# Causal attention and a gated MLP on one core: score maxima taken bank by bank, and a table that ranks every operation of the list schedule

## The chip, the cores and the metric

The kernel runs on one core of a Trainium2 chip. The metric is device time in microseconds of one execution. Three runs of the kernel before gave 362.40, 362.74 and 361.01 us, median 362.4. PE is TensorE (matmuls), DVE is VectorE, ACT is ScalarE, POOL is GpSimd, SP is the engine that issues the DMAs.

## What is computed

Four batches, twelve heads of 64, 448 tokens. Attention is causal; its output is the input x (448 x 768 per batch) of a gated MLP:

```python
scores = q @ k.T / sqrt(64);  scores[mask] = -1e9
attn = exp(scores - max);  attn = attn / sum;  x = attn @ v     # per head
h = gelu(x @ w_in);  u, v = h[..., :512], h[..., 512:]           # tanh gelu, 768 -> 1024
v_n = (v - mean) / sqrt(var + 1e-6) * g_ln
v_s = w_sg @ v_n + b_sg                                           # over tokens, 448 x 448
out = x + (u * v_s) @ w_out                                       # 512 -> 768
```

## The kernel before

The work is cut into operations of one to about ten instructions. Each is recorded by `od.add` with its engine, a modelled duration, what it reads and writes, and a number `at`. When all are recorded, `Order.plan` (line 157) makes a list schedule of them: it keeps a modelled clock for each engine, and when an engine is free it takes, of the operations that the model calls ready, the one with the lowest `at`. The instructions are then emitted in that order, and each engine runs its own instructions strictly in it; what an engine waits for is set by semaphores on the chip, not by the model. `STAY` (line 83) is added to `at` where PE would have to change the shape of its matmuls.

- **Pairs.** 24 pairs of heads, six per batch (`pair`, line 500). A pair loads q and k, and PE makes scores for four chunks of query rows (`CH`, line 24) in two groups: chunks 3 and 0 into one PSUM bank per head, chunks 2 and 1 into another (`GROUPS`). DVE adds the mask in place and takes the row maxima (`mxs`, line 528, eight per pair), ACT takes the exponentials with row sums (line 538, ten per pair), and DVE and a small PE transpose make the reciprocals of the sums, which go through DRAM to be spread (`rd`, `rb`). The exponentials are transposed: in pairs 0 to 7 by PE (`tx`, `ty`, line 585), then copied to SBUF by ACT or DVE (`evict`); from pair 8 on by DVE (line 573) and four DMAs. Then PE multiplies by v (`PV`, line 616), DVE scales the result (`scale`, line 646), and `keep_x` splits it into two parts for the MLP with ACT or POOL and POOL.
- **MLP.** Per batch (`mlp`, line 694), every operand is split in two parts and each product takes three matmuls. One operation of `group` (line 669) is three matmuls (`CUT`), for the token groups and the u groups those of one pair's x. First four token groups (`m<-win,x`, 512 columns), then four u groups (`m<-x,win`), four groups over tokens (`m<-wsg,vn`), and six output groups (`m<-g,wout`). Behind each stand gelu and normalisation on ACT, DVE and POOL. An operation that opens a PSUM bank for the MLP may run early (`EARLY = 2` of them) before all it needs is there.
- **Weights.** w_in comes in twelve pieces as 64-bit numbers and is converted by ACT (line 453), DVE (lines 455 and 457) and POOL (lines 460 and 461); w_out likewise in sixteen.
- **Start.** DVE clears a buffer (`warm`, line 422) and PE does seven matmuls on it (line 427) ahead of the first scores; DVE also clears constants (`consts2`, lines 407 to 413).
- **End.** The last output group of the last batch is added and stored in two halves (`cuts`).

What sets the order before is about a hundred numbers: `STEP`, `MLP`, `LEN`, `PAIR` and `DUE`, from which each operation's `at` is computed.

Of the kernel before, what the change touches and what calls it, by code (L numbers as in the profile page):

```python
# [23 lines left out]
CH = {  # L24
    3: (128, 448, 0, 0, 320),
    0: (64, 64, 0, 448, 0),
    2: (128, 320, 1, 192, 192),
    1: (128, 192, 1, 0, 64),
}
# [23 lines left out]
WO = 192  # L53

GROUPS = (3, 0), (2, 1)

WARM, FILL, EARLY = 7, 0, 2

# [10 lines left out]
    S=(351.19, -329.08, 282.5, 225.63), mx=(-8.77, -147.73, 166.31, -265.1),  # L69
# [10 lines left out]


TICK, BUSY, SHIFT = 10.24 / 3, 3400, 0.12
STAY = 286.72
MOVE = 0.62
FULL = 128, 128
COLD = 6.0, 1.35


def due(k, b):
    d = DUE[k]  # L90
    return d[b] if isinstance(d, tuple) else d
# [15 lines left out]
class Order:  # L107
# [49 lines left out]
    def plan(self):  # L157
# [61 lines left out]
        def when(n):  # L219
            t = rdy[n]  # L220
            for k, tag in enumerate(ops[n]["shr"]):
                if len(avail[tag]) <= k or len(avail[None]) <= k:
                    return 1e9
                if n in wants and stuck(n):
                    opened[:] = [m for m in opened if stuck(m)]
                    if len(opened) >= self.early[tag]:
                        return 1e9
                t = max(t, sorted(avail[tag])[k], sorted(avail[None])[k])
            return t
# [19 lines left out]
        while len(order) < len(ops):  # L249
# [10 lines left out]
            tops = [(ops[n]["at"], n) for n in banks if when(n) <= s + 1e-6] + [q[0] for q in now.values() if q]  # L260
            at, n = min(tops, key=lambda x: (x[0] + (STAY if e == "pe" and (ops[x[1]]["shape"] == FULL) != (shape == FULL) else 0.0), x[1]))
            o = ops[n]
# [18 lines left out]
            if e == "sp":  # L281

                moved = max(moved, end + 0.65) + o["size"] * (COLD[1] if end < COLD[0] else 1.0)
                done = moved + 1.5
# [29 lines left out]
def attention_gated_mlp(ctx: ExitStack, tc: tile.TileContext, qk, vP, w_in, g_ln, w_sgT, b_sg, w_out, out):  # L314
    nc = tc.nc
    B, HP, D, S = vP.shape[0], vP.shape[1], vP.shape[4] // 2, qk.shape[3]
# [24 lines left out]
    def bank(tag):  # L341
        return Buf(ps, [128, 512], F32, tag, "b")
# [4 lines left out]
    mask = const.tile([128, S], BF16, name="mask")  # L347
    mask2 = const.tile([128, 320], BF16, name="mask2")
# [18 lines left out]
    od = Order(slots, BANKS, 8, dict(m=EARLY))  # L367
# [5 lines left out]
    def pe(dur, fn, r, w, at, shape=FULL, rows=1.0):  # L373
        od.add("pe", dur, fn, r, w, at, shape=shape, rows=rows)
# [4 lines left out]
    def dve(n, fn, r, w, at, rate=1.0417, done=0.0, port=False, ring=()):  # L379
        od.add("dve", 0.068 + n * rate / 1000, fn, r, w, at, done, port=port, ring=ring)  # L380
# [4 lines left out]
    def start(p):  # L385
        b, h = divmod(p, HP)
        return sum(STEP[:b]) * HP + STEP[min(b, B - 1)] * h
# [112 lines left out]
    def pair(p):  # L500
        b, hp = divmod(p, HP)
        T = start(p) + PAIR[p]
# [3 lines left out]
        s = [[bank("s") for k in range(2)] for z in range(2)]  # L506
# [4 lines left out]
        def score(cs):  # L511
            for c in cs:
                m, n, bk, col, q0 = CH[c]
                w = 128 if m == 128 else 66
                for z in range(2):
                    r = slice(64 * z, 64 * z + 64)
                    nc.tensor.matmul(out=s[z][bk].t[0:w, col:col + n], lhsT=qk_.t[r, 0, q0:q0 + w],  # L517
                                     rhs=qk_.t[r, 1, 0:n], start=True, stop=True)
        for cs in GROUPS:
            pe(sum(CH[c][1] * 4 / 2400 + 0.036 for c in cs), lambda cs=cs: score(cs), [qk_],  # L520
               [s[z][CH[cs[0]][2]] for z in range(2)], T + due("S", b), (64, 128))


        for c in (3, 0, 2, 1):
            m, n, bk, col, _ = CH[c]
            mk = mask2 if c == 2 else mask[:, S - n:S] if m == 128 else mask[0:m, S - 128:S - 64]
            for z in range(2):
                def mxs(c=c, m=m, n=n, bk=bk, col=col, z=z, mk=mk):
                    o = s[z][bk].t[0:m, col:col + n]
                    nc.vector.tensor_tensor_reduce(out=o, in0=o, in1=mk, scale=-0.125, scalar=3e38, op0=ALU.add,  # L530
                                                   op1=ALU.min, accum_out=ngm[ib[z]][c][0:m])
                dve(n + {0: 45, 1: 45, 2: 10, 3: 5}[c], mxs, ["mask"], [s[z][bk], ("ngm", ib[z], c)], T + due("mx", b), done=0.1)
        ip = p % NS
        for k, (c, r0, k0, n, off, kc) in enumerate(EX):
            m, _, bk, col, _ = CH[c]
# [284 lines left out]
    for b in range(B):  # L820
        for h in range(HP):
            pair(b * HP + h)
        if b == 0:
            weights_b()
        mlp(b)
    with tc.manual_schedule():
        od.run()

# [41 lines left out]
```

## Time and profile before

| | |
|---|---|
| median of three runs | 362.4 us |
| the profiled execution, its own time | 362.34 us |
| its span, first to last instruction | 360.6 us |
| PE busy | 341.9 us, 95% |
| DVE busy | 258.1 us, 72% |
| ACT busy | 200.8 us, 56% |
| POOL busy | 146.9 us, 41% |
| DMA, mean | 193 GB/s |

Busy time is the union of an engine's instructions. A matmul counts as busy until its modelled end, so a busy PE may still be slowed. The page cuts the span into forty slices of about 9 us, and other views give the same for any stretch, by line, by engine or in order of time. Time outside the span is 1.7 us.

### The profile page before, as it was taken

What the parts mean: (1) busy time and instruction counts of PE and PEld (TensorE: products, weight loads), DVE (VectorE), ACT (ScalarE), POOL (GpSimd) and SP (SyncE); (2) the same over time, 40 slices, a digit from 0 to 9 for tenths busy, and PEclk for the clock granted to TensorE, in tenths of its full rate; (3) what the DMA queues carried; (4) which work ended last, traced back from release to release, by engine and by line L of the source; (5) the groups of instructions that cost most, each with busy time, mean ns of one, the idle gap of its engine ahead of it and who ended that gap; (6) DMA issues with size and microseconds to landing.
All of it is one profiled execution on the core that took longest, in us unless ns stands there. A gap on an engine that the chain in (4) does not pass through costs nothing.

```text
span 360.6 us, 6952 instructions
## 1 busy us (share of the span) xinstructions
PE 341.9 (95%) x2231; PEld 271.3 (75%) x2231; DVE 258.1 (72%) x801; ACT 200.8 (56%) x658; POOL 146.9 (41%) x185
## 2 busy tenths in 40 slices
PE   7797999899999999899999989999999999999995
PEld 3464655577889778688978678776888898889994
DVE  6689898699999878738278977778976551286521
ACT  3999999794676186363147855454761600245210
POOL 2227785647557863003421831104235700333630
PEclk9699999899999999999999999999999999999999
DMA  7958999797766547896049589896751668400023
GB/s 243 339 170 264 294 293 336 264 333 220 227 180 211 145 127 189 254 282 192 2 131 273 157 238 273 266 287 187 199 157 31 164 175 246 154 2 0 0 77 128
DMA packets 37972, 69.50 MB, mean 193 GB/s; under 512 B 3888, under 2 KB 18992, under 8 KB 37936
## 3 DMA queue, kind: packets, MB, share of 16 engines
q1 hardware_dynamic: 37936, 69.06, 63.0%
q8 instruction: 18, 0.29, 0.3%
q14 instruction: 18, 0.15, 0.1%
HBM read 39.68 MB, written 12.58 MB: 145 GB/s over the span
## 4 chain that ended last, share of the span: by engine, by line
PE 71%; DVE 10%; DMA 9%; ACT 5%; SPq 3%; issue 1%; DVEq 0%; ACTq 0%
PE m L677 46%; PE o L616 11%; PE s L517 9%; DVE s L530 4%; ACT P L538 3%; DMA B<-P 3%; DMA res<-xd 3%; SPq L577 2%; PE tx L585 2%; PE ty L585 2%; DVE P L573 1%; DMA qk<-in_qk_dram 1%; DMA vraw<-in_vP_dram 1%; DMA xd<-xt 1%; DVE ngm L530 1%
## 5 line engine op out<-in xcount | busy, mean ns | idle before, releaser
L538 ACT ACTIVATE P<-s,ngm 64x64 f32<-64x64 f32 (+3 forms) x240 | 100.2, 426 | 33.5 <-DVE ngm L530 31.4
L530 DVE CUSTOM_DVE_ANT_0 s<-s,mask 128x448 f32<-128x448 f32 (+2 forms) x192 | 75.4, 445 | 12.0 <-PE s L517 11.7
L677 PE MATMUL m<-g,wout 128*128 128x448 f32 x288 | 62.0, 370 | 0.2 <-ACT P L538 0.2
L677 PE MATMUL m<-win,x 128*128 128x512 f32 (+1 forms) x264 | 61.9, 392 | 0.0
L677 PE MATMUL m<-x,win 128*128 128x448 f32 x288 | 60.4, 367 | 0.0
L677 PEld LDWEIGHTS m<-x,win 128*128 128x128 f32 x288 | 53.7, 188 | 5.0 <-issue 0.5
L677 PEld LDWEIGHTS m<-g,wout 128*128 128x128 f32 x288 | 53.0, 188 | 5.7 <-ACT P L538 0.6
L677 PEld LDWEIGHTS m<-win,x 128*128 128x128 f32 (+1 forms) x264 | 47.9, 183 | 11.8
L658 POOL TENSOR_TENSOR x<-xt,x 128x448 fp32r<-128x448 f32 x24 | 27.8, 1167 | 67.1 <-ACT x L657 63.6
L517 PE MATMUL s<-qk 64*128 64x192 f32 (+3 forms) x384 | 54.7, 408 | 0.4 <-DVE tmp L778 0.4
L616 PE MATMUL o<-B,vraw 128*64 128x64 f32 (+4 forms) x672 | 48.3, 293 | 3.3 <-DMA B<-P 1.9
L573 DVE STREAM_TRANSPOSE P<-P 128x1024 f32<-128x1024 f32 x32 | 39.2, 1229 | 14.6 <-DMA B<-P 13.0
L517 PEld LDWEIGHTS s<-qk 64*128 64x128 f32 (+1 forms) x384 | 32.6, 178 | 22.1 <-issue 13.0
L538 ACT ACTIVATION_READ_ACCUMULATOR P<-s,ngm 128x1 f32 (+1 forms) x240 | 47.6, 198 | 0.0
L616 PEld LDWEIGHTS o<-B,vraw 128*64 128x64 f32 x672 | 33.6, 137 | 18.1 <-issue 5.6
L677 PE MATMUL m<-wsg,vn 128*128 128x448 f32 x176 | 36.8, 366 | 0.0
L677 PEld LDWEIGHTS m<-wsg,vn 128*128 128x128 f32 x176 | 32.9, 188 | 2.8 <-issue 0.2
L808 DVE TENSOR_TENSOR res<-m,res 128x448 f32<-128x448 f32 (+1 forms) x25 | 14.7, 598 | 24.8 <-PE m L677 14.1
L731 POOL TENSOR_TENSOR mv<-mv,mhalf 128x1 f32<-128x1 f32 (+1 forms) x16 | 9.1, 570 | 52.3 <-DVE mv L729 52.3
L688 ACT ACTIVATE tmp<-tmp 128x448 f32<-128x448 f32 (+2 forms) x32 | 19.1, 605 | 18.1 <-DVE tmp L686 18.0
L657 ACT ACTIVATE x<-xt 128x448 fp32r<-128x448 f32 x18 | 10.1, 574 | 29.4 <-DVE xt L646 27.2
L530 DVE DVE_READ_ACCUMULATOR2_ANT ngm<- 128x1 f32 (+1 forms) x192 | 26.0, 135 | 0.0
(72 smaller groups left out, 385.7 us busy)
## 6 DMA issues: line engine op xcount, KB each, us to landing
B<-P SPq DMA_DIRECT2D x64, 256.0 KB
qk<-in_qk_dram SPq DMA_DIRECT2D x24, 448.0 KB
vn<-in_w_in_dram SPq DMA_DIRECT2D x12, 512.0 KB
vraw<-in_vP_dram SPq DMA_DIRECT2D x24, 256.0 KB
rb<-rd SPq DMA_DIRECT2D x24, 256.0 KB
xd<-xt SPq DMA_DIRECT2D x24, 224.0 KB
res<-xd SPq DMA_DIRECT2D x12, 448.0 KB
out_dram<-res SPq DMA_DIRECT2D x9, 448.0 KB
```

The costliest lines, as they stand in the source:

```text
L517: nc.tensor.matmul(out=s[z][bk].t[0:w, col:col + n], lhsT=qk_.t[r, 0, q0:q0 + w], rhs=qk_.t[r, 1, 0:n], start=True, stop=True)
L530: nc.vector.tensor_tensor_reduce(out=o, in0=o, in1=mk, scale=-0.125, scalar=3e38, op0=ALU.add, op1=ALU.min, accum_out=ngm[ib[z]][c][0:m])
L538: act(n, lambda c=c, m=m, r0=r0, k0=k0, n=n, bk=bk, col=col, off=off, kc=kc, i=i, z=z: nc.scalar.activation(out=P[i][r0:m, off:off + n], i ...
L573: dve(PW, lambda z=z: nc.vector.transpose(A[ia][:, :, :, z, :].rearrange("p g t k -> p t g k"), P[ib[z]]), Pk[z] + ["P"], Ak, Tt, 1.105)
L585: nc.tensor.transpose(out, P[ib[z]][:, col:col + 128], ident)
L616: nc.tensor.matmul(out=dst(o.t[r]), lhsT=vr.t[:, c, r], rhs=src(z), start=first and n == 0, stop=last and n == len(lst) - 1)
L657: act(S, lambda: nc.scalar.activation(out=y.t[:, 0:S], in_=x.t, func=AF.Copy), [x], [y], Ty, True)
L658: pool_tt(S, lambda: nc.gpsimd.tensor_tensor(out=y.t[:, S + 64:], in0=x.t, in1=f(y.t)[:, 0:S], op=ALU.subtract), [x, y], [(y, 1)], Ty)
L677: nc.tensor.matmul(out=ps.t[0:l().shape[1], 0:n], lhsT=l(), rhs=rr(), start=(k == 0), stop=(k == len(mms) - 1))
L688: act(n, lambda: nc.scalar.activation(out=z(), in_=z(), func=AF.Tanh, scale=GS * GC), [], [t], at, True)
L731: od.add("pool", 0.46, lambda mv=mv, m=m: nc.gpsimd.tensor_tensor(out=mv.t[0:m, 1:2], in0=mv.t[0:m, 1:2], in1=mhalf[0:m], op=ALU.pow), ["s ...
L808: dve(hi - lo, lambda rr=rr, ps=ps, z=z, lo=lo, hi=hi: nc.vector.tensor_tensor(out=rr.t[:, z, lo:hi], in0=ps.t[:, lo:hi], in1=rr.t[:, z, l ...
```

## The change

Two edits. The maxima of a pair are recorded bank by bank and head by head with the narrow chunk first (`MX`): chunk 0 then 3 of head 0, then of head 1, then chunk 1 then 2 likewise. And after all operations are recorded, `at` of each is replaced by its place in a table of all 1926 of them, `ORDER`; `STAY` becomes 0. The numbers that made `at` before no longer decide anything but the numbering. The planner's model and its rules of readiness, buffers and banks stay.

```diff
+MX = (0, 3), (1, 2)
...
-STAY = 286.72
+STAY = 0.0
...
+ORDER = (
+    0, 1, 83, 11, 117, 127, 3, 2, 171, 17, 4, 23, 5, 6, 347, 7, 161, 8, 9, 10, 84, 85, 88, 12, 86, 13, 87, 215, 90,
...
+)
...
-               [s[z][CH[cs[0]][2]] for z in range(2)], T + due("S", b), (64, 128))
+               [s[z][k] for k in sorted({CH[c][2] for c in cs}) for z in range(2)], T + due("S", b), (64, 128))
...
-        for c in (3, 0, 2, 1):
-            m, n, bk, col, _ = CH[c]
-            mk = mask2 if c == 2 else mask[:, S - n:S] if m == 128 else mask[0:m, S - 128:S - 64]
-            for z in range(2):
+        for cs in MX:
+            for z, c in [(z, c) for z in range(2) for c in cs]:
+                m, n, bk, col, _ = CH[c]
+                mk = mask2 if c == 2 else mask[:, S - n:S] if m == 128 else mask[0:m, S - 128:S - 64]
...
+    for k, n in enumerate(ORDER):
+        od.ops[n]["at"] = k
```

Each score group wrote one bank per head already, so the third edit changes nothing. No operation is added or removed. Lines of the changed kernel are 101 to 104 higher than before, behind the table.

**DVE, start of the program.** Before:

```order
L422 MEMSET tmp 128x512
L407 MEMSET P_90 128x64 x4
L407 MEMSET P_91 128x64 x4
L407 MEMSET P_92 128x64 x4
...
L412 MEMSET mhalf 128x1
L413 MEMSET wsg 64x448
L530 ISA s,ngm_96<-s,mask 128x448
```

Now:

```order
L508 MEMSET P_90 128x64 x4
L508 MEMSET P_91 128x64 x4
L508 MEMSET P_92 128x64 x4
...
L513 MEMSET mhalf 128x1
L514 MEMSET wsg 64x448
L523 MEMSET tmp 128x512
L632 ISA s,ngm_97<-s,mask 64x64
```

The clearing of `tmp`, on which the seven first matmuls of PE wait, moved behind all fourteen rows of constants.

**PE, around the scores of pair 5** (`o<-B,vraw` is PV, `s<-qk` scores, `tx` and `ty` transposes, `m<-win,x` the MLP's token groups). Before:

```order
L616 MATMUL o<-B,vraw 64x320 x2
L616 MATMUL o<-B,vraw 64x64 x2
L616 MATMUL o<-B,vraw 64x128 x2
L616 MATMUL o<-B,vraw 64x64 x2
L552 MATMUL s<-ident,rs 8x128
L517 MATMUL s<-qk 128x448 x2
L517 MATMUL s<-qk 66x64 x2
L517 MATMUL s<-qk 128x320 x2
L517 MATMUL s<-qk 128x192 x2
```

Now:

```order
L718 MATMUL o<-B,vraw 64x64 x2
L779 MATMUL m<-win,x 128x512 x3
L654 MATMUL s<-ident,rs 8x128
L618 MATMUL s<-qk 128x320 x2
L618 MATMUL s<-qk 128x192 x2
L687 MATMUL tx<-ident,P_91 128x2x64
L687 MATMUL tx<-ident,P_91 128x128 x3
L687 MATMUL ty<-ident,P_91 128x2x64
L687 MATMUL ty<-ident,P_91 128x128 x3
L779 MATMUL m<-win,x 128x512 x3
L718 MATMUL o<-B,vraw 64x448 x2
```

Matmuls of the first MLP now stand between the parts of pairs 2 to 7. Before, the first of them stands behind PV of pair 7; now 72 of the token groups and 24 of the u groups stand ahead of it.

**PE, where the first MLP goes from its third kind of group to its fourth.** Before:

```order
L616 MATMUL o<-B,vraw 64x64 x4
L552 MATMUL s<-ident,rs 8x128
L677 MATMUL m<-g,wout 128x448 x6
L517 MATMUL s<-qk 128x448 x2
L517 MATMUL s<-qk 66x64 x2
L677 MATMUL m<-g,wout 128x448 x12
```

Now:

```order
L779 MATMUL m<-wsg,vn_1476 128x448 x2
L779 MATMUL m<-g,wout 128x448 x6
L618 MATMUL s<-qk 128x448 x2
L618 MATMUL s<-qk 66x64 x2
L618 MATMUL s<-qk 128x320 x2
L618 MATMUL s<-qk 128x192 x2
L654 MATMUL s<-ident,rs 8x128
L779 MATMUL m<-g,wout 128x448 x39
```

PV of pairs 10 and 11, which stood ahead of the first `m<-g,wout`, moved behind 60 of its 72 matmuls, together.

## Rows read from the trace of the kernel before

**Rows 1.** The page: busy time, share of span, instructions.

```profile
PE 341.9 (95%) x2231; PEld 271.3 (75%) x2231; DVE 258.1 (72%) x801; ACT 200.8 (56%) x658; POOL 146.9 (41%) x185
```

**Rows 2.** Stretches: span, busy us (instructions) of each engine, granted clock, DMA share, GB/s.

```profile
8.00:75.00 67.00, 58.69 (x439) 37.36 (x436) 55.44 (x217) 63.60 (x232) 37.01 (x42) 0.92 0.85 283
74.70:120.00 45.30, 45.30 (x271) 38.13 (x269) 44.53 (x122) 28.94 (x91) 30.67 (x46) 1.00 0.72 216
0.00:126.40 126.40, 116.26 (x792) 82.20 (x792) 109.06 (x383) 95.86 (x326) 75.57 (x105) 0.96 0.79 251
120.00:150.00 30.00, 28.27 (x224) 21.56 (x224) 22.62 (x77) 14.84 (x56) 14.14 (x17) 1.00 0.67 194
205.00:250.00 45.00, 42.40 (x292) 33.03 (x292) 33.83 (x104) 24.33 (x88) 11.27 (x13) 1.00 0.86 250
```

**Rows 3.** In order of time, first 9 us: start, duration, what [idle before it <-releaser].

```profile
0.91 0.48 DVE L422 MEMSET tmp<- 128x512 uint32 x1 [0.91 <-PEq L859]
...
3.54 0.43 DVE L413 MEMSET wsg<- 64x448 f32 x1
...
5.84 0.63 DVE L530 CUSTOM_DVE_ANT_0 s<-s,mask 128x448 f32<-128x448 f32 x1 [1.87 <-PE s L517]
...
1.45 3.17 PE L427 MATMUL m<-tmp 128*128 128x512 bf16 x7 [1.45 <-DVE tmp L422]
...
4.55 3.84 PE L517 MATMUL s<-qk 64*128 64x448 f32 x32
...
7.46 0.63 ACT L538 ACTIVATE P<-s,ngm 128x448 f32<-128x448 f32 x1 [3.83 <-DVE ngm L530]
```

**Rows 4.** By line: names, shapes xcount | busy us, mean ns | idle before <-releasers. ACT.

```profile
L538 ACT ACTIVATE P<-s,ngm 64x64 f32<-64x64 f32 (+3 forms) x240 | 100.2, 426 | 33.5 <-DVE ngm L530 31.4 <-DVE P L573 0.5 <-PE m L677 0.2
...
L592 ACT ACTIVATE B<-tx 128x512 f32<-128x512 f32 x16 | 9.5, 595 | 1.7 <-PE tx L585 1.6
...
L453 ACT ACTIVATE vn<-vn 128x512 f32<-128x512 f32 x12 | 8.0, 680 | 0.1
...
L453 ACT ACTIVATE g<-g 128x192 f32<-128x192 f32 x16 | 5.3, 378 | 1.5 <-DMA g<-in_w_out_dram 0.9 <-POOL wout L461 0.6
...
L688 ACT ACTIVATE tmp<-tmp 128x448 f32<-128x448 f32 (+2 forms) x32 | 19.1, 605 | 18.1 <-DVE tmp L686 18.0
```

**Rows 5.** In order of time: the last copy of pair 7 on ACT, then PE.

```profile
69.64 0.60 ACT L592 ACTIVATE B<-ty 128x512 f32<-128x512 f32 x1
...
71.62 2.08 PE L616 MATMUL o<-B,vraw 128*64 128x448 f32 x24
```

**Rows 6.** By line: PE, the token groups, the u groups, the scores and PV.

```profile
L677 PE MATMUL m<-win,x 128*128 128x512 f32 (+1 forms) x264 | 61.9, 392 | 0.0
...
L677 PE MATMUL m<-x,win 128*128 128x448 f32 x288 | 60.4, 367 | 0.0
...
L517 PE MATMUL s<-qk 64*128 64x192 f32 (+3 forms) x384 | 54.7, 408 | 0.4 <-DVE tmp L778 0.4
...
L616 PE MATMUL o<-B,vraw 128*64 128x64 f32 (+4 forms) x672 | 48.3, 293 | 3.3 <-DMA B<-P 1.9 <-DMA xd<-xt 1.0
```

**Rows 7.** Stretches at half clock, columns as in rows 2.

```profile
11.30:18.10 6.80, 5.71 (x24) 4.13 (x23) 4.00 (x18) 6.67 (x29) 1.93 (x2) 0.50 0.87 317
65.90:69.30 3.40, 3.40 (x15) 2.38 (x16) 1.72 (x8) 1.75 (x8) 3.32 (x4) 0.50 0.51 149
```

**Rows 8.** DVE: by line, the transposes; in order of time, the fourth gcol step.

```profile
L573 DVE STREAM_TRANSPOSE P<-P 128x1024 f32<-128x1024 f32 x32 | 39.2, 1229 | 14.6 <-DMA B<-P 13.0 <-ACT P L538 1.6
...
125.72 0.68 DVE L778 SCALAR_TENSOR_TENSOR tmp<-m,gcol,bB 128x448 f32<-128x448 f32 x1
```

**Rows 9.** One line on DVE: count, min/median/max ns, first and last start; then POOL by line.

```profile
L455 DVE TENSOR_SCALAR g<-g x16: 213/350/875, 78.4 to 118.4; 128x192 int32<-128x192 int32 x16
L455 DVE TENSOR_SCALAR vn<-vn x12: 379/420/1367, 10.1 to 76.3; 128x512 int32<-128x512 int32 x12
...
L461 POOL TENSOR_TENSOR win<-vn,win 128x512 fp32r<-128x512 f32 x12 | 16.7, 1389 | 0.9
```

95 rows, old and new, of the table ORDER are left out of this document.

## The prediction

> **What bounds the kernel now.** The page says PE, 95% busy [rows 1], but that is an average over stages with different limits, so I read the stretches next [rows 2]. From 8 to 75 us, while pairs 0 to 7 go through, PE is busy 58.69 of 67 us and ACT 63.60: ACT is the engine without room, and PE waits for its exponentials and copies. From 74.7 to 120 us, the first MLP, PE is full but so is DVE, 44.53 of 45.3 us. Only after that do both ACT and DVE have room, and what PE still loses there is 1.73 us between 120 and 150 and 2.60 us between 205 and 250. So the kernel has about 8 us of idle PE in a stretch where it has no matmuls that may run, and behind it a stretch that DVE would not let run much faster. Last come the lines of ACT and PE, which give prices [rows 4, 6], and the first microseconds in order of time [rows 3].
>
> **The change, part by part.** The sum is made against the profiled execution, 362.34 us, a span of 360.6 us and 1.7 us around it; the median of the runs is 362.4 us, the same. A difference of 0.5%, 1.8 us, is about what the measurement can tell from none.
>
> *Start: 2.5 us later.* The constants on DVE take from 1.39 us, where the clearing of `tmp` ends, to 3.97 us, 2.58 us [rows 3]. They now come first, so PE's first matmul moves from 1.45 to about 4.0 us. Its seven take 3.1 us to the first score, which moves from 4.55 to 7.1 us. DVE's first maximum moves from 5.84 to 8.4 us. There the narrow chunk goes first; two maxima of 64 columns and one step of weight unpacking (at least 0.379 us [rows 9]) stand ahead of the first wide one. I take ACT's first exponential at 10.0 us instead of 7.46. This is the price of one moved operation, and nothing hides it, as ACT is the limit next.
>
> *Pairs 0 to 7: 9.8 us ahead at their end.* Ahead of the last copy of pair 7, ACT now has 92 exponentials, 26 copies, 4 weight pieces like copies, 11 conversions of w_in (the twelfth falls into ACT's wait at the start), 10 of w_out and 6 gelu steps of the MLP. From the rows [rows 4]: 92 x 100.2/240 = 38.4, 30 x 0.595 = 17.9, 11 x 8.0/12 = 7.3, 10 x 5.3/16 = 3.3, 6 x 0.605 = 3.6, together 70.5 us. The same count for the kernel before (87, 30 and 10) gives 60.9 us from 7.46 us, so 68.4 us, where the trace has 70.24 [rows 5]: ACT waited 1.9 us. With that wait the change ends there at 10.0 + 70.5 + 1.9 = 82.4 us, and PV of pair 7, which before ended 3.5 us behind this copy (at 73.70 us [rows 5]), ends at 85.9 us. By then PE has also done 72 matmuls of the token groups and 24 of the u groups, which before came afterwards: 72 x 61.9/264 + 24 x 60.4/288 = 16.9 + 5.0 = 21.9 us [rows 6]. Before, the same work was done at 73.7 + 21.9 = 95.6 us. PE has the room: its 8.3 idle us, and the second stretch at half clock. In that stretch, 65.9 to 69.3 us, the granted clock is 0.50, that is 1.2 instead of 2.4 GHz, and PE before it had waited and done scores and transposes [rows 7]; half of 3.4 us is lost. The first such stretch, 11.3 to 18.1 us, comes before any MLP matmul can run, and stays.
>
> *First MLP: DVE takes part of the lead back.* Up to the end of the fourth `tmp<-m,gcol` step of the first MLP (line 778), at 126.4 us [rows 8], DVE was busy 109.06 us and idle 17.3 [rows 2]. In the change DVE has the same work ahead of that step but for the transposes of pair 11 (2 x 1.229 us [rows 8]) and some 0.6 us of maxima: 106.0 us. Of the idle time 5.4 us cannot go: 0.9 at the start and 4.5 between the last start-up clearing (now at 4.0 us) and the first maximum. So the bound for this step is 111.4 us. Between that and no lead at all lies the other 14.5 us of DVE's idle time, of which 11.6 fell between 8 and 75 us, where DVE waited for ACT's pace. As ACT stays the limit there I let half remain, 7.3 us: the step ends at 118.7, 7.7 us earlier. That is less than the 9.8 of PE, so DVE decides. But PE then owes work that before was done: PV of pair 10 (48.3/24 = 2.0 us) and scores of pair 12 (54.7/24 = 2.3 us) [rows 6]. What is left is 3.4 us. Ends: nothing to 10.7 us (111.4).
>
> *Later stages: 2.2 us.* PV of pairs 10 and 11, and later 13 and 14, 16 and 17, now stand together and far behind the DMAs that they wait for, with output and token groups between. PE's idle time in the two stretches is 4.3 us [rows 2]; the new order may remove it or make as much again, as DVE's transposes also stand in other places. I take half as gain. Between 250 and 351 us PE is full and nothing can be won. At the end, the last add is now a whole group instead of half; no row parts its store from the rest, so I set it at nothing, and 0.6 us either way.
>
> *Maxima bank by bank: nothing.* Same instructions. The first exponential of a head needs two maxima instead of three, but ACT has no room from 8 to 75 us, so what comes earlier waits in its queue. If ACT's queue were empty it would be worth one wide maximum, 0.63 us, per pair.
>
> Sum: -3.4 - 2.2 = -5.6, so 362.3 - 5.6 = **356.7 us**.
>
> **A rule against it.** One unpacking step on DVE took 1367 ns where its least is 379, about as long as one POOL subtraction, 1389 [rows 9]; the twelve and the sixteen lose 12 x (535 - 379) and 16 x (405 - 213) ns by their means, some 5 us, in a stretch where POOL was busy 37 of 67 us [rows 2]. The Trainium skill, "SBUF — State Buffer", section "Who interferes with whom", says why: VectorE's fast one-input modes, and its instructions with two SBUF inputs, share a port pair with GpSimd, and the second to come waits for the whole instruction of the first. By that rule packing both engines tighter lengthens DVE, and if these 5 us doubled the sum would be near 361 us; the trace agrees with the rule in that one step, and shows nothing of how often it will meet.
>
> **The rivals.**
> 1. *The lead is kept whole* (0.18). DVE's idle time between 8 and 75 us closes, as the exponentials of one head now come together and its transposes start sooner. For it: DVE is 98% busy in the next stretch and so can be driven that hard. Against: ACT is the limit in that stretch. Price: 10.7 + 4.3 = 15 us at most, half of the way beyond my value about 350 us.
> 2. *DVE gives nothing* (0.14). It is full from 74.7 to 120 us already, and its unpacking steps, of which one took 1367 ns for 379 [rows 9], lose up to the same 5 us again when POOL works beside them. The lead of PE ends in waits for gelu and normalisation: about 361 us.
> 3. *Slower: a matmul of the MLP holds up the pairs* (0.18). PE takes its instructions in order. At seven places ahead of the end of PV of pair 5, MLP matmuls stand in front of scores and transposes that feed DVE and ACT. They need x of pairs 0 to 4 and the pieces of w_in, both made by POOL, where one piece costs 1.39 us and a cast besides. If each place holds PE for more than 0.8 us beyond ACT's lead, the gain of 5.6 us is gone; at 1.3 us each, 9.1 us lost, the time is 366 us. Against it: PE has some 12% of room in the stretch, and POOL was busy only 37 of 67 us there [rows 2]. For it: no row shows these waits, since before no MLP matmul ran before 74.7 us.
>
> That the order on the chip is not the table's is no rival: the emitted streams differ as the rows of the change show.
>
> **How the numbers follow.** The forecast has 0.50, with times from 351 to 360 us. Rival 1 lies below, rival 2 nearly all within 0.5% of 362.3 (360.5 to 364.1), rival 3 nearly all above. So faster 0.50 + 0.18 + 0.01 = 0.69, same 0.13, slower 0.18. A range that leaves out about a third of rival 1 below and somewhat over half of rival 3 above is 348 to 364.5 us.
>
> **What would show it.** Right: the first score at about 7.1 us and the first exponential near 10; the last copy of pair 7 on ACT near 82 us with ACT over 95% busy up to it; no half clock after the first stretch; the fourth `tmp<-m,gcol` step near 119 us; DVE near full from 85 to 119; PE idle less than 4 us behind it. Wrong: idle time in front of `m<-win,x` before 80 us (rival 3), mean times of the unpacking steps well over 535 and 405 ns (rival 2), or the last copy of pair 7 later than 88 us.

## The result, and the profile after

The changed kernel takes 359.27 us, the median of six runs (357.52 to 359.93); the kernel before, beside it, 362.03 us (361.01 to 363.08). The ratio is 0.9918, with a 95% interval of 0.9889 to 0.9947: 2.8 us faster, where 5.6 were forecast. The profiled execution took 359.28 us, its span is 357.5 us, 3.1 us less than before. A run over 1.5% above the fastest of its kernel is left out of the medians and ratios here and below (one of the six of the fill experiment, 367.61 us, and one of the kernel before, 365.66 us).

The page after has PE busy for 1.4 us more than [rows 1], and yet for a larger share:

```profile
PE 343.3 (96%) x2231; PEld 269.9 (75%) x2231; DVE 258.7 (72%) x801; ACT 204.2 (57%) x658; POOL 148.9 (42%) x185
```

So the idle time of PE fell from 18.7 us (360.6 - 341.9) to 14.2 (357.5 - 343.3). The view by stretches says where. Its columns are those of [rows 2]: span, busy us of PE, PEld, DVE, ACT and POOL, granted clock, DMA share, GB/s. The kernel before:

```profile
0.00:8.00 8.00, 6.55 (x37) 3.20 (x39) 4.56 (x35) 2.03 (x4) 2.62 (x11) 1.00 0.71 232
8.00:45.00 37.00, 31.27 (x222) 20.16 (x219) 30.64 (x127) 36.60 (x138) 17.84 (x19) 0.91 0.82 269
45.00:75.00 30.00, 27.42 (x219) 17.20 (x218) 24.79 (x91) 26.99 (x96) 19.16 (x24) 0.94 0.89 300
75.00:125.00 50.00, 49.94 (x315) 40.96 (x313) 47.66 (x129) 30.23 (x93) 34.89 (x51) 1.00 0.73 214
125.00:160.00 35.00, 33.33 (x222) 26.65 (x223) 23.81 (x89) 20.80 (x86) 9.92 (x12) 1.00 0.71 206
```

The changed kernel, the same stretches and the one from 205 us:

```profile
0.00:8.00 8.00, 3.88 (x9) 1.39 (x11) 2.46 (x24) 2.15 (x3) 2.63 (x11) 1.00 0.75 241
8.00:45.00 37.00, 32.40 (x201) 19.29 (x198) 29.55 (x121) 32.42 (x118) 17.32 (x17) 0.91 0.72 247
45.00:75.00 30.00, 29.77 (x224) 20.14 (x226) 23.83 (x84) 26.59 (x90) 22.23 (x27) 1.00 0.86 280
75.00:125.00 50.00, 50.00 (x329) 40.32 (x327) 48.29 (x149) 36.61 (x116) 38.40 (x57) 1.00 0.73 214
125.00:160.00 35.00, 34.68 (x237) 27.18 (x234) 28.76 (x100) 23.34 (x92) 6.09 (x8) 1.00 0.81 229
205.00:250.00 45.00, 44.40 (x335) 35.03 (x332) 32.97 (x100) 19.39 (x74) 7.81 (x10) 1.00 0.73 212
```

Span less PE's busy time gives the account, before and after (the last stretch of before from [rows 2]):

| stretch | idle before | idle after | gained |
|---|---|---|---|
| 0 to 8 us, the start | 1.45 | 4.12 | -2.67 |
| 8 to 45 us, pairs | 5.73 | 4.60 | 1.13 |
| 45 to 75 us, pairs | 2.58 | 0.23 | 2.35 |
| 75 to 125 us, first MLP | 0.06 | 0.00 | 0.06 |
| 125 to 160 us | 1.67 | 0.32 | 1.35 |
| 205 to 250 us | 2.60 | 0.60 | 2.00 |
| all else, the end with it | 4.61 | 4.33 | 0.28 |

Together 4.5 us less idle, and 1.4 us more busy: 3.1 us. Of the 3.48 us that the two lines of the pairs gain, the start takes 2.67; what is left comes mostly from behind 125 us.

The first microseconds after, in order of time (start, duration, idle time before it and what ended it):

```profile
3.58 0.48 DVE L523 MEMSET tmp<- 128x512 uint32 x1 [0.15 <-issue]
...
4.12 3.17 PE L528 MATMUL m<-tmp 128*128 128x512 bf16 x7 [4.12 <-DVE tmp L523]
...
7.22 5.04 PE L618 MATMUL s<-qk 64*128 64x448 f32 x30
9.50 0.23 DVE L632 CUSTOM_DVE_ANT_0 s<-s,mask 64x64 f32<-64x64 f32 x1 [5.44 <-PE s L618]
...
10.95 0.64 ACT L640 ACTIVATE P<-s,ngm 128x448 f32<-128x448 f32 x1 [3.80 <-DVE ngm L632]
```

The first score comes at 7.22 us, as forecast (7.1); the first exponential at 10.95, where 10.0 was forecast and 7.46 stands before [rows 3]. In a second profile of the same program (the experiment "the change again") it comes where it was forecast:

```profile
9.92 0.63 ACT L640 ACTIVATE P<-s,ngm 128x448 f32<-128x448 f32 x1 [2.82 <-DVE ngm L632]
```

Three more landmarks of the changed kernel: the last copy of pair 7 on ACT, PV of pair 7 on PE, and the fourth step of the first MLP with `gcol` on DVE:

```profile
92.25 0.60 ACT L694 ACTIVATE B<-ty 128x512 f32<-128x512 f32 x1 [0.45 <-PE ty L687]
...
93.81 1.96 PE L718 MATMUL o<-B,vraw 128*64 128x448 f32 x20
...
123.59 0.68 DVE L880 SCALAR_TENSOR_TENSOR tmp<-m,gcol,bB 128x448 f32<-128x448 f32 x1
```

Forecast were 82.4 us for the copy, 85.9 for the end of PV (it ends at 95.8) and 118.7 for the end of the step (124.3). By 95.8 us PE has also done 96 matmuls of the first MLP; the prediction put the same work before at 95.6 us. In this execution the change has no lead at all at this point. In the second profile PV of pair 7 ends at 93.4 us, with 3.4 us at half clock in place of 6.8: about 2 us of lead, against the 9.7 (95.6 - 85.9) that were forecast.

### The profile page after: what moved, and what is told of

It reads as the page before. It is cut to its first block, busy times and chain, and to the rows that moved or that the text cites. A ratio compares the mean times of both kernels' runs of the same rounds, so it can differ in the third digit from the quotient of the medians.

```text
span 357.5 us, 6919 instructions
## 1 busy us (share of the span) xinstructions
PE 343.3 (96%) x2231; PEld 269.9 (75%) x2231; DVE 258.7 (72%) x801; ACT 204.2 (57%) x658; POOL 148.9 (42%) x185
## 4 chain that ended last, share of the span: by engine, by line
PE 55%; ACT 15%; issue 11%; DVE 8%; DMA 5%; POOL 3%; SPq 2%; DVEq 0%; ACTq 0%; POOLq 0%
PE m L779 41%; ACT P L640 11%; PE s L618 6%; PE o L718 5%; DMA B<-P 5%; DVE P L675 2%; DVE s L632 2%; SPq L679 2%; ACT B L694 2%; PE tx L687 1%; PE ty L687 1%; POOL tmp L884 1%; POOL x L760 1%; PE m L528 1%; ACT vn L554 1%
## 5 line engine op out<-in xcount | busy, mean ns | idle before, releaser
L640 ACT ACTIVATE P<-s,ngm 128x448 f32<-128x448 f32 (+3 forms) x240 | 101.0, 426 | 40.1 <-DVE ngm L632 26.5
L632 DVE CUSTOM_DVE_ANT_0 s<-s,mask 128x192 f32<-128x192 f32 (+3 forms) x192 | 75.2, 444 | 14.6 <-PE s L618 10.5
L779 PE MATMUL m<-win,x 128*128 128x512 f32 (+1 forms) x264 | 66.3, 397 | 0.3 <-ACT P L640 0.3
L779 PE MATMUL m<-x,win 128*128 128x448 f32 x288 | 63.6, 370 | 0.3
L779 PE MATMUL m<-g,wout 128*128 128x448 f32 x288 | 63.1, 369 | 0.4 <-ACT P L640 0.4
L618 PE MATMUL s<-qk 64*66 64x64 f32 (+3 forms) x384 | 55.7, 412 | 2.7 <-ACT P L640 2.3
L618 PEld LDWEIGHTS s<-qk 64*128 64x128 f32 (+1 forms) x384 | 33.5, 182 | 25.4 <-issue 13.9
L640 ACT ACTIVATION_READ_ACCUMULATOR P<-s,ngm 128x1 f32 (+1 forms) x240 | 46.9, 195 | 0.0
L779 PE MATMUL m<-wsg,vn 128*128 128x448 f32 x176 | 39.0, 369 | 0.0
L760 POOL TENSOR_TENSOR x<-xt,x 128x448 fp32r<-128x448 f32 x24 | 28.8, 1205 | 22.3 <-ACT x L759 12.6
L884 POOL TENSOR_TENSOR tmp<-tmp,g 128x448 f32<-128x448 f32 x16 | 18.3, 1150 | 20.1 <-DVE tmp L880 20.0
L787 ACT ACTIVATE tmp<-m 128x448 f32<-128x448 f32 (+1 forms) x28 | 15.4, 565 | 18.9 <-PE m L779 17.4
L632 DVE DVE_READ_ACCUMULATOR2_ANT ngm<- 128x1 f32 (+1 forms) x192 | 25.7, 134 | 0.0
```

Of the source, the lines that this page charges most:

```text
L640: act(n, lambda c=c, m=m, r0=r0, k0=k0, n=n, bk=bk, col=col, off=off, kc=kc, i=i, z=z: nc.scalar.activation(out=P[i][r0:m, off:off + n], i ...
L760: pool_tt(S, lambda: nc.gpsimd.tensor_tensor(out=y.t[:, S + 64:], in0=x.t, in1=f(y.t)[:, 0:S], op=ALU.subtract), [x, y], [(y, 1)], Ty)
L779: nc.tensor.matmul(out=ps.t[0:l().shape[1], 0:n], lhsT=l(), rhs=rr(), start=(k == 0), stop=(k == len(mms) - 1))
L787: act(n, lambda: nc.scalar.activation(out=z(), in_=h(), func=AF.Square), [ps], [t], at)
L884: pool_tt(S, lambda z=z, u=u: nc.gpsimd.tensor_tensor(out=z(), in0=z(), in1=u.t, op=ALU.mult), [u], [t], at)
```

## The experiments

Each kernel emits the operations of one of the two kernels in its own order, written out as a list, so that nothing moves but what the edit names:

```diff
-        for n in self.plan():
+        for n in ORDER:
             self.ops[n]["fn"]()
```

The diffs below show the rows of the emitted streams. Ratios are to the kernel before, run beside each; 0.01 is 3.6 us.

### The change again

No edit; the list is the changed kernel's own.

> The changed kernel itself, its order written out, beside the other two of this call, so that they are compared on one chip. Every theory expects the ratio of the first measurement, 0.989 to 0.995.

Measured: 0.9904 (0.9878 to 0.9931), six runs from 356.06 to 359.56 us. The profiled one was among the fastest, with a span of 354.9 us; why is told at the end.

### The start: tmp cleared first

```diff
+L523 MEMSET tmp 128x512
 L508 MEMSET P_90 128x64 x4
...
 L514 MEMSET wsg 64x448
-L523 MEMSET tmp 128x512
```

> The changed kernel in its emitted order, with one operation moved: DVE clears tmp ahead of the constants again. Theory A (the head is a fixed loss): the first exponential of the change came at 10.95 us instead of 7.46, and with ACT the limit up to about 45 us these 3.5 us are carried to the end; the time is about 355.8 us (359.3 - 3.5). Theory B (the head is mostly made up): the last matmul of PV of pair 0 ends only 0.7 us later in the change than before (27.2 against 26.5), so the rest is slack of the pairs; about 358.6 us. Either way the first score is expected near 4.6 us and the first exponential near 8.3.

Measured: 0.9862 (0.9841 to 0.9883), 356.03 us, faster than both kernels. Against the 0.9904 to 0.9918 of the change this is 1.5 to 2.0 us, between the two theories. The first score comes at 4.55 us and the first exponential at 8.29:

```profile
4.55 2.95 PE L618 MATMUL s<-qk 64*128 64x448 f32 x16
...
8.29 0.63 ACT L640 ACTIVATE P<-s,ngm 128x448 f32<-128x448 f32 x1 [1.04 <-DVE ngm L632]
```

PV of pair 7 ends at 91.9 us, 3.9 us earlier than in the first profile of the change. Against its second profile the first exponential comes 1.6 us earlier (8.29 for 9.92), PV of pair 7 1.5 us (91.9 for 93.4) and the end of the span 0.4 us (354.5 for 354.9): the pairs carry the delay on, and a part of it is made up behind them. Behind 250 us PE idles for 1.44 us instead of 0.37 in the first profile: PV of pair 22 now comes before its DMA has landed (1.1 us). How much of the 1.5 to 2.0 us is the start itself and how much the half clock, of which this profile has none, is not separated: the two runs of the change again with the highest mean clock, 0.995, took 356.06 and 356.63 us, hardly longer than the five here (355.39 to 356.29).

### The start: the same move in the kernel before

```diff
-L422 MEMSET tmp 128x512
 L407 MEMSET P_90 128x64 x4
...
 L413 MEMSET wsg 64x448
+L422 MEMSET tmp 128x512
```

> The kernel before in its emitted order, with the same operation moved the other way: the constants on DVE ahead of the clearing of tmp. Theory A: 3.5 us later, 365.5 us (362.0 + 3.5). The prediction's own term: 2.5 us, 364.5 us. Theory B (made up behind): under 1 us, 362.7. The first score is expected at about 7.2 us.

Measured: 1.0096 (1.0073 to 1.0118), 364.07 us, 3.5 us slower. Theory A; the first exponential moved from 7.46 to 10.47 us. In this kernel nothing behind it hides the start.

### The fill: ten operations of the first MLP behind the pairs

```diff
-L779 MATMUL m<-win,x 128x512 x3
 L654 MATMUL s<-ident,rs 8x128
 L618 MATMUL s<-qk 128x320 x2
...
 L718 MATMUL o<-B,vraw 64x64 x2
+L779 MATMUL m<-win,x 128x512 x30
```

> The changed kernel in its emitted order, with ten operations of the first MLP's token groups (30 matmuls, 30 x 0.228 = 6.8 us of PE's time at their distance) taken from between the pairs 4 to 7 and put behind the last PV of pair 6, in front of the ones that stand there. Theory A (they fill PE's idle time there, which was 2.6 of 30 us before between 45 and 75 us, and keep the clock up): without them PE idles again and the half-clock stretch returns, and the time rises by 2 to 4 us, to 361.3 to 363.3. Rival (rival 3 of the prediction in a mild form: they hold up scores and so ACT, which waited 7.5 us for maxima between 11 and 93 us): the pairs go faster without them and the time falls by 1 to 3 us, to 356.3 to 358.3.

Measured: 1.0088 (1.0047 to 1.0128), 363.92 us, some 6 us slower than the change: theory A, and more than it said. Between 45 and 75 us PE is idle for 5.37 us, where the change has 0.23:

```profile
45.00:75.00 30.00, 24.63 (x211) 15.63 (x210) 25.39 (x94) 26.17 (x91) 23.51 (x28) 1.00 0.87 282
```

The half-clock stretch did not return there, so that part of the theory fell. The last PV matmuls in front of the moved ones start 1.6 us earlier than in the change, here and there:

```profile
74.09 1.21 PE L718 MATMUL o<-B,vraw 128*64 128x320 f32 x16
```

```profile
75.67 1.21 PE L718 MATMUL o<-B,vraw 128*64 128x320 f32 x16
```

0.3 us of this was there at 43 us already. So without 6.8 us of matmuls between them the pairs go 1.2 us faster, and the rest of that time PE stands idle: the matmuls hold the pairs up a little and fill idle time for the most. PV of pair 7, which stands behind the moved matmuls, ends at 101.0 us instead of 95.8.

### The maxima in the changed kernel

What DVE does turned out to differ from the order in which the maxima are recorded. Of the 48 groups (two per pair) only 6 go head by head on DVE in the changed kernel; 32 go narrow, narrow, wide, wide, with the heads in the same order, and 10 with the heads in the other order for the wide ones. Before, all 48 go wide, wide, narrow, narrow. So what the first edit changes on DVE is narrow before wide, and the words "head by head" in the expectations below describe the recorded order only. Three kernels put the wide ones first again. The first:

```diff
-L632 ISA s,ngm_101<-s,mask 64x64
-L632 ISA s,ngm_105<-s,mask 64x64
 L632 ISA s,ngm_104<-s,mask 128x448
 L632 ISA s,ngm_108<-s,mask 128x448
+L632 ISA s,ngm_101<-s,mask 64x64
+L632 ISA s,ngm_105<-s,mask 64x64
```

> The changed kernel in its emitted order, with the maxima of every pair put back as before within each bank pair: the wide chunk of both heads, then the narrow one (chunk 3 of both heads, then 0; chunk 2 of both, then 1). Theory A (the prediction's term): nothing, 359.3 within 1 us. Rival 1: bank by bank helps ACT start a head's exponentials, so the time rises by up to 0.63 us for each pair in which ACT's queue is empty, to some 361 us. Rival 2: the narrow maximum ahead of the wide one only delays the first, wide exponential, so the time falls by about 1 us, to 358.3.

Measured: 1.0344 (1.0320 to 1.0369), 373.23 us, far outside all three. Not a clean test: some narrow maxima stood behind an exponential that reads the same bank, and DVE waited there for ACT (7.7 us in nine waits of L632, where the change has 3.9 in four). The second keeps every exponential behind both maxima of its bank (same diff for this group):

> The changed kernel in its emitted order, with the first edit undone: at the four places of each bank pair the wide maxima of both heads go first, then the narrow ones, and a head's exponentials stand behind both maxima of their bank, as the kernel before records them (one group, of pair 16, keeps the new order, because the table puts an MLP step between its places). In the wide-first experiment some narrow maxima stood behind an exponential that reads the same bank, and DVE waited for ACT; here none does. Theory A (the prediction's term): nothing, 359.3 us, a ratio to the kernel before of 0.989 to 0.995. Rival (the two edits hang together: the table puts other DVE work between the places of the two heads, and ACT waited 19 times for maxima): the first head's exponentials now wait for the third place and not the second, 0.2 us or more at each of the 19 waits, and the time rises by 3 to 6 us, a ratio near 1.00.

Measured: 1.0154 (1.0129 to 1.0178), 366.69 us, 8.5 us slower than the change. The prediction's "nothing" fell. ACT's idle time ahead of the exponentials grew by 8.2 us, its waits for maxima in it by 9.7; the changed kernel first, then this one (line, names, count | busy, mean ns | idle time before and what ended it):

```profile
L640 ACT ACTIVATE P<-s,ngm 128x448 f32<-128x448 f32 (+3 forms) x240 | 101.0, 426 | 40.1 <-DVE ngm L632 26.5 <-DVE P L675 6.4 <-DVE mv L830 2.0
```

```profile
L640 ACT ACTIVATE P<-s,ngm 128x448 f32<-128x448 f32 (+3 forms) x240 | 100.8, 425 | 48.3 <-DVE ngm L632 36.2 <-DVE P L675 6.3 <-DVE mv L830 2.0
```

The profile also shows more half clock, a granted clock of 0.83 from 8 to 45 us where the change has 0.91. In the 10 groups with the heads in the other order, though, this kernel also moved one head's last maximum from the third place to the fourth, and in the 6 that go head by head the first head's from the second to the third. The third kernel swaps narrow and wide within each head, so that each head is complete at the same place as in the change:

```diff
-L632 ISA s,ngm_101<-s,mask 64x64
-L632 ISA s,ngm_105<-s,mask 64x64
-L632 ISA s,ngm_104<-s,mask 128x448
-L632 ISA s,ngm_108<-s,mask 128x448
-L632 ISA s,ngm_102<-s,mask 128x192
+L632 ISA s,ngm_104<-s,mask 128x448
+L632 ISA s,ngm_108<-s,mask 128x448
+L632 ISA s,ngm_101<-s,mask 64x64
+L632 ISA s,ngm_105<-s,mask 64x64
+L632 ISA s,ngm_103<-s,mask_83 128x320
...
```

> The changed kernel in its emitted order, with one half of the first edit undone: the maxima stay head by head, but within a head the wide chunk goes ahead of the narrow one, at the same two places, in all 48 groups. Undoing the whole edit gave a ratio of 1.015 to the kernel before, where the change has 0.992. Theory A (going head by head is what counts; a head's exponentials stand behind both maxima of their bank anyway): nothing, a ratio of 0.989 to 0.995, about 359.3 us. Rival (narrow first is what counts): most of the 1.015, about 366 us.

Measured: 1.0022 (1.0000 to 1.0043), 362.11 us, about 4 us slower than the change: the rival, at half its size. One place where ACT waits shows how it can come about, in order of time. The changed kernel:

```profile
75.00 0.37 DVE L632 CUSTOM_DVE_ANT_0 s<-s,mask 128x192 f32<-128x192 f32 x1 [0.72 <-PE s L618]
...
76.22 0.53 ACT L640 ACTIVATE P<-s,ngm 128x320 f32<-128x320 f32 x1 [1.77 <-DVE ngm L632]
```

And with the wide ones first:

```profile
75.34 0.50 DVE L632 CUSTOM_DVE_ANT_0 s<-s,mask 128x320 f32<-128x320 f32 x1 [0.57 <-PE s L618]
...
76.70 0.53 ACT L640 ACTIVATE P<-s,ngm 128x320 f32<-128x320 f32 x1 [1.76 <-DVE ngm L632]
```

The first head's exponentials start behind the third place of four. From the first maximum to the first exponential it is 1.22 us in the changed kernel, two narrow and one wide, and 1.36 us here, two wide and one narrow. Over the whole run ACT's idle time ahead of the exponentials is 4.4 us longer than in the change (44.5 us for 40.1):

```profile
L640 ACT ACTIVATE P<-s,ngm 128x448 f32<-128x448 f32 (+3 forms) x240 | 100.9, 425 | 44.5 <-DVE ngm L632 26.5 <-DVE P L675 7.1 <-PE s L618 3.8
```

The 26.5 us put down to maxima are the same in both only because the wait of 3.8 us ahead of the first exponential is put down to the scores here and to the maxima there. That the small step, where ACT has no queue, makes up the 4 us is an inference; the loss is spread over the stages.

### The maxima alone, in the kernel before

Two tries, at the places where the maxima stood. Head by head, in all 48 groups:

```diff
-L632 ISA s,ngm_104<-s,mask 128x448
-L632 ISA s,ngm_108<-s,mask 128x448
 L632 ISA s,ngm_101<-s,mask 64x64
+L632 ISA s,ngm_104<-s,mask 128x448
 L632 ISA s,ngm_105<-s,mask 64x64
+L632 ISA s,ngm_108<-s,mask 128x448
```

> The kernel before in its emitted order, with the first edit alone: at the four places on DVE where a bank pair's maxima stood, they now go narrow then wide of one head, then of the other. Theory A (the prediction's term): nothing, a ratio to the kernel before of 0.997 to 1.003, about 362.0 us. Rival: the exponential of the first head waits for two maxima and not three; ACT waited 17 times for maxima before, and if each of these waits before 75 us (4.5 us in all) loses up to one wide maximum of 0.63 us, some 2 us are gained, 360.0 us.

Measured: 1.0070 (1.0042 to 1.0097), 363.74 us: slower, which neither expected. Its profile has one more stretch at half clock than that of the kernel before (129.4 to 132.7 us, granted clock 0.50), which may be a part of it. And as most groups go in the changed kernel:

```diff
-L632 ISA s,ngm_104<-s,mask 128x448
-L632 ISA s,ngm_108<-s,mask 128x448
 L632 ISA s,ngm_101<-s,mask 64x64
 L632 ISA s,ngm_105<-s,mask 64x64
+L632 ISA s,ngm_104<-s,mask 128x448
+L632 ISA s,ngm_108<-s,mask 128x448
```

> The kernel before in its emitted order, with the maxima of each of the 48 groups in the order that DVE has in 32 of the changed kernel's: the narrow ones of both heads, then the wide ones of both, at the same four places. (In the earlier try the two heads went one after the other, which only 6 groups of the changed kernel do.) The exponentials of the first head stand behind both maxima of their bank, so they may start behind the third place: by the steps from one maximum to the next in the changed kernel's trace (0.15, 0.32, 0.45 and 0.55 us for 64, 192, 320 and 448 columns) that is 0.55 - 0.15 = 0.40 us earlier in one group of a pair and 0.45 - 0.32 = 0.13 us in the other. Theory A (narrow first pays wherever ACT waits for maxima): 0.5 to 2 us faster than the kernel before, a ratio of 0.994 to 0.999. Rival (the order of the kernel before was found with the wide ones first, and its ACT takes the heads by turns, so that the second head's wait decides): no gain or a loss as in the earlier try, a ratio of 1.000 to 1.008.

Measured: 1.0020 (0.9995 to 1.0045), 362.17 us: no gain, the rival. In its trace the waits put down to maxima are shorter than before, 21.4 us for 31.4 [rows 4], but ACT's idle time ahead of the exponentials is not, 37.3 us for 33.5; the rest is put down to other steps:

```profile
L640 ACT ACTIVATE P<-s,ngm 64x64 f32<-64x64 f32 (+3 forms) x240 | 100.4, 428 | 37.3 <-DVE ngm L632 21.4 <-PE s L654 4.5 <-PE s L618 4.4
```

So the first edit is worth nothing by itself, and taking it out of the changed order costs 4 us or more. A rival to "narrow first pays in this table" is left: each order may have been fitted to its own maxima, so that most moves inside it cost. Narrow first made the kernel before no faster and wide first made the changed one slower, as this rival would have it too; no run here parts the two.

### The two orders spliced

Up to the first `m<-g,wout` of the first MLP the one, from there the other:

```diff
-ORDER = changed
+ORDER = before[:860] + [n for n in changed if n not in before[:860]]
```

> The order of the kernel before, old maxima included, up to the first m<-g,wout operation of the first MLP (860 of 1926 operations), and from there the changed kernel's order. Theory A (the gain of the change lies mostly behind this point: of PE's time there it lost about 3 us less than before between 125 and 350 us, while its start and its pairs gave nothing net): about 3 us faster than the kernel before, 359.0 us, a ratio of 0.99. Rival (the later gain hangs on the state that the table's first part hands over, with PV of pairs 10 and 11 still owed): no gain, 362.0 us, a ratio of 1.00.

Measured: 1.0111 (1.0084 to 1.0137), 364.97 us. And the reverse:

```diff
-ORDER = changed
+ORDER = changed[:821] + [n for n in before if n not in changed[:821]]
```

> The changed kernel's order up to the first m<-g,wout operation of the first MLP (821 of 1926 operations), and from there the order of the kernel before, with its old maxima. Theory A: the first part gives nothing net (its lost start is paid by the filled pairs), so the time is that of the kernel before, 362.0 us, a ratio of 1.00. Rival (the prediction's: the first part carries the gain, 3.4 of 5.6 us): about 359 us, a ratio of 0.99.

Measured: 1.0316 (1.0282 to 1.0351), 371.98 us. Neither theory holds in either kernel, and these runs can't say which half carries the gain, because the seam costs more. In the second kernel PE comes to PV of pairs 10 and 11 at once, and waits there in its order for a DMA and for DVE, with the half clock behind it (granted clock 0.80 from 125 to 160 us):

```profile
127.64 3.69 PE L718 MATMUL o<-B,vraw 128*64 128x256 f32 x32 [4.23 <-DMA B<-P]
137.57 1.73 PE L718 MATMUL o<-B,vraw 128*64 128x256 f32 x11 [3.46 <-DVE ngm L632]
```

The changed kernel does these two PV from 139.7 us on, behind output matmuls, and waits for nothing. That is its gain between 125 and 160 us. That it could not have it without the early MLP matmuls, which bring the output matmuls forward, is argued and not shown. Behind the seam the order does tell: from 160 to 250 us PE idles for 1.45 us under the changed kernel's order and 2.35 under the one of before; in the two kernels themselves it is 0.75 and 2.73.

### A version from the findings

On the experiment with tmp cleared first: the first MLP operation ahead of PV of pair 2, with x of pair 0 made earlier and steps of the weights' unpacking put behind it, and two output operations ahead of PV of pair 22.

```diff
+L779 MATMUL m<-win,x 128x512 x3
 L718 MATMUL o<-B,vraw 64x448 x2
...
 L718 MATMUL o<-B,vraw 64x64 x2
-L779 MATMUL m<-win,x 128x512 x3
...
+L779 MATMUL m<-g,wout 128x448 x6
 L718 MATMUL o<-B,vraw 64x256 x2
```

> The experiment with the clearing of tmp first, and two places where PE still waited there mended: the scaling of pair 0 (DVE) and its x (POOL) some 5 us earlier, so that the first token-group operation of the MLP stands ahead of PV of pair 2 (PE waited 0.62 us there), and two output operations of batch 2 ahead of PV of pair 22 (PE waited 1.1 us there for a DMA). Theory A (PE's idle time anywhere behind the first MLP matmul is worth its length): 1.0 to 1.7 us off that experiment's ratio of 0.986, a ratio of 0.981 to 0.983, about 354.5 us. Rival (the waits move on to the next place): a ratio of 0.986.

Measured: 0.9845 (0.9831 to 0.9860), 355.90 us, the fastest of all; 2.1 us ahead of the changed kernel run beside it (0.9904). Against tmp first alone (0.9862) the gain is 0.6 us, and the intervals overlap. PE's idle time from 250 to 300 us fell from 1.44 to 0.35 us and from 8 to 45 us from 5.94 to 4.40, but the second kernel has a half-clock stretch in its profile that the first has not; whether the waits were worth their length stays open.

## Why the prediction was right, and half off

*Start, 2.5 us: right in the first exponential.* It came 2.5 us later in the second profile and 3.5 in the first. To the end the start cost 3.5 us in the kernel before, and at most the 1.5 to 2.0 us by which clearing `tmp` first shortens the changed one.

*Pairs 0 to 7, 9.8 us ahead at their end: the step that failed.* The term took the last copy of pair 7 as set by ACT's work. That work was right to a tenth, 70.5 us forecast and 70.46 measured between the first exponential and that copy; the same count gave 60.9 us for the kernel before, where the trace has 59.60, so the tenth is luck. But the wait, taken as the 1.9 us of before, was wrong: ACT idled for 11.4 us (81.9 - 70.46), and in the kernel before not for 1.9 but for 3.2 (62.78 - 59.60). It was busy for 86% and not for over 95%, and the copy ended at 92.9 us, beyond the 88 us that the prediction names as a sign of being wrong. The kernel before, then the change, and the change from 75 us on:

```profile
7.46:70.24 62.78, 54.47 (x399) 34.81 (x397) 52.02 (x210) 59.60 (x215) 37.01 (x42) 0.92 0.84 280
```

```profile
11.00:92.90 81.90, 77.07 (x511) 51.99 (x507) 69.07 (x253) 70.46 (x242) 51.81 (x66) 0.96 0.80 258
75.00:92.90 17.90, 17.90 (x105) 14.45 (x103) 17.19 (x56) 11.50 (x36) 12.26 (x24) 1.00 0.89 268
```

Of ACT's 11.4 idle us 6.4 (17.90 - 11.50) lie behind 75 us, where PE has no idle time at all. What set the last copy there was PE's order. The last exponential of pair 7 ends at 71.4 us, but of its four groups of transposes three stand behind 51 matmuls of the MLP and more, through which PE runs without a gap; the copies wait for them:

```profile
71.06 0.31 ACT L640 ACTIVATE P<-s,ngm 64x64 f32<-64x64 f32 x1
...
76.80 4.41 PE L779 MATMUL m<-win,x 128*128 128x512 f32 x18
...
81.08 4.35 PE L779 MATMUL m<-win,x 128*128 128x512 f32 x18
85.27 3.20 PE L779 MATMUL m<-x,win 128*128 128x448 f32 x15
88.31 0.60 PE L687 MATMUL ty<-ident,P 128*128 128x128 f32 x4
...
91.62 0.60 PE L687 MATMUL ty<-ident,P 128*128 128x128 f32 x4
```

ACT's longest sums of waits between 12 us and that copy (engine, line and what it waited for: us in total, times, longest). The 7.5 us for maxima that the expectation of the fill experiment gives have the wait of 3.8 us ahead of the first exponential in them:

```profile
ACT P L640 <- DVE ngm L632: 3.7, 4, 1.8
ACT tmp L790 <- DVE tmp L788: 2.7, 3, 1.1
ACT B L694 <- PE tx L687: 1.9, 3, 0.8
```

The premise behind the term, "PE has the room: its 8.3 idle us", counted idle time that the MLP's matmuls could not reach. Of those 8.3 us 5.7 lie before 45 us, and in the changed order the x of pair 0, which the first `m<-win,x` needs, is ready on POOL at 43.6 us and the matmul stands at 46.9. Behind 45 us there were 2.6 us of idle PE and 1.7 of half clock, 4.3 us, and into these went 21.9 us of matmuls by the prediction's sum. So PE filled up (29.77 of 30 us, then 50.00 of 50) and took ACT's place as the limit. Of the room 2.35 us of idle time was won, and the second half-clock stretch went, as forecast; the start took most of it back.

*First MLP, 3.4 us: by another way.* The fourth `gcol` step came 2.1 us earlier (124.3 for 126.4), where 7.7 were forecast. PE brought no lead for DVE to take back: from 75 to 125 us PE was full, and DVE had 1.7 us left (48.29 of 50). In the working, the "other 14.5 us" of DVE's idle time is not 17.3 less the 5.4 named there, which would be 11.9; it comes out as 17.3 less the 2.8 us that DVE idled at the start before (0.91 + 1.87 [rows 3]).

*Later stages, 2.2 us: right in place, larger in size.* The two stretches named then, 120 to 150 and 205 to 250 us, had 4.3 us of idle PE and now have 0.9 (0.32 and 0.60): 3.4 us won where half was forecast, and the end gained 0.7 us (from PE's last matmul to the end of the span 4.5 us before, 3.8 now). About 1.4 us went back into PE's busy time, though half clock fell by one stretch: the token groups' matmuls, now mixed with others, take 397 ns in the mean for 392 [rows 6], the scores 412 for 408; what lengthened them is not shown.

*Maxima, nothing: right alone, open in the table.* Alone nothing or a loss; undone inside the table, a loss of 4 us or more, be it for narrow before wide or for a fitted order disturbed. The prediction took the recorded order for DVE's.

*The rivals.* Rival 1, the lead kept whole, has next to no lead to keep. Rival 3, PE waiting at matmuls of the MLP and so holding up the pairs, did not happen: the waits in front of `m<-win,x` before 80 us are 0.0 us in the trace, and without ten of these operations the pairs go only 1.2 us faster and the kernel is slower. Rival 2's sign was half there: one kind of unpacking step went from 535 to 695 ns, but the four kinds together fell. Before:

```profile
L457 DVE SCALAR_TENSOR_TENSOR vn<-vn 128x512 int32<-128x512 int32 x12 | 9.5, 794 | 0.5 <-ACT vn L453 0.4
L457 DVE SCALAR_TENSOR_TENSOR g<-g 128x192 int32<-128x192 int32 x16 | 7.4, 484 | 0.0
L455 DVE TENSOR_SCALAR vn<-vn 128x512 int32<-128x512 int32 x12 | 6.3, 535 | 0.0
L455 DVE TENSOR_SCALAR g<-g 128x192 int32<-128x192 int32 x16 | 6.1, 405 | 0.0
```

After:

```profile
L556 DVE TENSOR_SCALAR vn<-vn 128x512 int32<-128x512 int32 x12 | 8.3, 695 | 0.2 <-DMA vn<-in_w_in_dram 0.2
L558 DVE SCALAR_TENSOR_TENSOR vn<-vn 128x512 int32<-128x512 int32 x12 | 8.1, 678 | 0.8 <-ACT vn L554 0.6
L558 DVE SCALAR_TENSOR_TENSOR g<-g 128x192 int32<-128x192 int32 x16 | 6.1, 401 | 0.0
L556 DVE TENSOR_SCALAR g<-g 128x192 int32<-128x192 int32 x16 | 4.4, 296 | 0.0
```

That is 29.3 us before and 26.9 after, with POOL busier (39.55 us from 8 to 75 us, for 37.01). The 5 us lost in these steps did not double. The rule of the Trainium skill, "SBUF — State Buffer", section "Who interferes with whom", agrees with the one step of 1812 ns that the trace after has (from 51.23 us; POOL works on three instructions from 50.23 to 52.76 us, one behind the other); the rest of it no run here tests.

That the sum came out at half and not at nothing is in part luck: its largest term was not there, and the later stages, by more than was forecast for them, stood in for it.

## What to carry to other kernels

Idle time of the bounding engine is room only from the moment on at which the work that is to fill it can run: split it at the first time its inputs exist, and ask which engine is full once it is filled. Count, too, what stands ahead of a landmark on every engine's own stream: here a copy of ACT was late by what PE had in front of it. A step at the head of the program that frees the first matmul can be worth its length to the end, as in the kernel before. Two edits made together are to be tried apart and together, and what an engine does is read from its emitted stream, since the order in which operations are recorded need not be theirs.

## What was not expected of the hardware

The same program had half-clock stretches of different length from execution to execution. The changed kernel, profiled twice, first and then again (stretch, span, busy us, granted clock):

```profile
16.90:23.60 6.70, 6.20 (x25) 3.90 (x24) 3.59 (x13) 6.10 (x23) 2.31 (x2) 0.50 0.30 101
```

```profile
17.30:20.60 3.30, 3.30 (x16) 2.58 (x16) 2.77 (x10) 3.26 (x12) 1.56 (x2) 0.50 0.05 10
```

The first of these executions has a span of 357.5 us, the second 354.9. With tmp cleared first the profile has no such stretch at all (granted clock 1.00 from 6.5 to 350 us, span 354.5). Of the six runs of the change taken again, the two shortest (356.06 and 356.63 us) have a mean granted clock of 0.995 and the other four (357.89 to 359.56) one of 0.989 or 0.990. So part of the 2 to 4 us by which runs of one kernel differ goes with the time that PE spends at 1.2 GHz, and a difference of that size between two single profiles says nothing about an edit.
